# A third arm for expert slots of 33 to 64 rows: raw weights in two column tiles of 64

## The chip, the cores and the metric

The kernel runs on one core of one Trainium2 chip, as one program with one launch. The metric is the device time of an execution in microseconds (us).

## What is computed

Three blocks follow each other. The reference, cut to the block that the change touches:

```python
def reference(...):
    attn_out = _attn_ref(...)                      # (4, 8, 544, 64): local and global attention
    x = attn_out.transpose(0, 2, 1, 3).reshape(B, S, H * D)
    x = _moe_ref(x, w_gate, w_local, w1, w2)
    return _moe2_ref(x, w_in, conv_w, w_out)       # dense layer, convolution, gate, dense layer

def _moe_ref(x, w_gate, w_local, w1, w2):          # x (4, 544, 512), 8 experts
    logits = x @ w_gate
    local_gate = sigmoid(x @ w_local)
    for b in range(B):
        for s in range(S):
            e = argmax(logits[b, s]) if s == 0 or local_gate[b, s] < 0.5 else prev_e
            prev_e = e
            p = softmax(logits[b, s])
            h = maximum(x[b, s] @ w1[e], 0.0)      # w1[e] is 512 x 1024
            out[b, s] = p[e] * (h @ w2[e])         # w2[e] is 1024 x 512
```

All data are float32. There are 2,176 tokens. With the reference's inputs the experts 0 to 7 get 412, 308, 241, 397, 261, 158, 382 and 17 of them.

## The kernel before, in words

**The expert block.** After attention the routing sorts tokens by expert into *slots* of up to 128 rows. There are NSLOT = 25 slots, of which 22 are in use here. Slots 0 and 1 (NA = 2) are full slots of expert 0; their routing needs the first half of the tokens alone. The second routing phase (`phase_b`, L844) places the rest: the experts follow each other, and the first slot of each is the one that isn't full. Its rows stand at the end of the 128 rows, the last partitions. A small integer table `esi` holds per slot the expert, whether the expert changes there (row 1), what to load next (rows 2 and 3) and a flag for a short slot (row 5). `few` (L937) computes that flag on VectorE from the number of empty rows of each expert's first slot: 1 where at most 32 rows are filled.

**The order of the work.** `Moe.step` (L1452) is written out by hand. For slot s it issues, in this order: the flag of slot s + 1 (`small`, L1343), layer 1 of slot s (`layer1`, L1386), the load of the next layer 1 weights where an expert has begun (`fetch`, L1325), the gather of slot s + 3, the transposes of slot s + 1's rows (`turn_x`, L1354), a load of 512 columns of the third block's weights, the split of slot s + 1's layer 1 weights (`resplit`, L1337), layer 2 of slot s - 1 (`layer2`, L1439) with the scatter of its result, the load of the next layer 2 weights, the transposes of slot s's hidden rows (`turn_h`, L1424), and the split of slot s's layer 2 weights. Each engine works through its own part of this order. One piece per step of the third block's weights is converted from 64-bit storage between these (`convert`, L1487), on ScalarE, VectorE and GpSimd. The last of the step loop's slots goes through `last` (L1208).

**Two arms.** A full slot multiplies in three products of split numbers. A weight is a high part `wh` (a ScalarE cast) and a low part `wl` (a VectorE subtraction), and so are the rows (`xh`, `xl` and, for the hidden rows, `gh`, `gl`); L1110 and L1126 are the three products of layer 1 and layer 2, with the full 128 x 128 array and 512 columns per matmul. A short slot multiplies the raw float32 numbers instead, straight from the buffers `ws` in which the weights land. Its 32 rows take 32 columns of the array, so four groups of output columns run side by side: `few_l1` (L1399) issues 4 x 4 matmuls of 256 columns, `few_l2` (L1413) 8 x 4 of 128 columns, and `few_turn` (L1407) two transposes where a full slot has eight. `either` (L1348) is the branch between the two; it stands on the TensorE, ScalarE and VectorE queues:

```python
def either(self, s, few, all_):
    with self.tc.If(self.sm[s] != 0) as c:
        few()
    with c.Else():
        all_()
```

The weight buffers `ws` exist once per layer. A load into one waits for all that read it, the raw arm's matmuls and the split alike.

**Around the first slots.** While `phase_b` runs on VectorE, TensorE works on slots 0 and 1 (`fill`). `few` is called between the last comparison that builds the index matmul's operand and the computation of the gather indices. Slot 2 is the first of the second phase, and its transposed rows are prepared in both forms, since its flag is still on the way.

Of the kernel before, what the change touches and what calls it, by code (L numbers as in the profile page):

```python
# [13 lines left out]
ALU = mybir.AluOpType  # L14
# [3 lines left out]
P = 128  # L18
B, H, SL, SG, DH = 4, 8, 512, 32, 64
S = SL + SG  # L20
DM = H * DH
# [538 lines left out]
NA = 2  # L560
# [95 lines left out]
class Routing:  # L656
# [327 lines left out]
PAD_C, PAD_F = 104, 8  # L984
TS = 32
NTS = P // TS
NWARM_M = 10
# [65 lines left out]
class Moe:  # L1053
# [154 lines left out]
    def last(self, s, cwr, cw):  # L1208
# [20 lines left out]
        r = nc.values_load(self.rt.esi[0:1, 5, s:s + 1], min_val=0, max_val=1,  # L1229
                           engines=[mybir.EngineType.Activation, mybir.EngineType.DVE])  # L1230
# [6 lines left out]
        with self.tc.If(self.sm[s] != 0):  # L1237
            self.few_l1(xs, hp, hs)
        self.turn_h(p)
# [8 lines left out]
        tq = self.px.tile([P, 4, P], F32, tag="tr", name="hlq")  # L1248
        self.either(s, lambda: self.few_turn(hs, tq), full1)
        self.conv_w(cwr, cw)  # L1250
# [23 lines left out]

        self.either(s, lambda: self.few_l2(hs, yp, y), full2)
        resplit(4, NFC)
# [66 lines left out]
    def small(self, s):  # L1343
        self.sm[s] = self.nc.values_load(self.rt.esi[0:1, 5, s:s + 1], min_val=0, max_val=1,
                                         engines=[mybir.EngineType.PE, mybir.EngineType.Activation,
                                                  mybir.EngineType.DVE])

    def either(self, s, few, all_):  # L1348
        with self.tc.If(self.sm[s] != 0) as c:
            few()  # L1350
        with c.Else():
            all_()

    def turn_x(self, s):  # L1354
        nc = self.nc
        xs = self.xs[s]
        x = self.xt[s] = tuple(self.tp.tile([P, NKC, P], F32R, tag="x" + q, name="x" + q) for q in "hl")
        t = (self.ps if s == NA else self.px).tile([P, 4, P], F32, tag="tr", name="xlp")
# [5 lines left out]
        def few():  # L1364
            turn()
            raw()

        def raw():
            nc.scalar.copy(xs[:, 0:NKC * TS].rearrange("p (k t) -> p k t", t=TS), t[:, :, P - TS:P])

        def split():
            nc.scalar.copy(x[0], t)
            self.lo_t(x, 0, t)

        def full():
            turn()
            split()

        if s == NA:
            turn()  # L1380
            raw()
            split()
        else:
            self.either(s, few, full)

    def layer1(self, s):  # L1386
        nc, W = self.nc, self.W
        x, xs, hp = self.xt.pop(s), self.xs.pop(s), self.h_tile()
        hs = self.hs[s] = self.tp.tile([P, FF], F32, tag="hs", name="hs")

        def full():
            for k in range(NKC):
                self.l1_mm(x, W.t[1], hp, k, range(2))
            for c in range(2):
                self.relu_c(hp, hs, c)

        self.either(s, lambda: self.few_l1(xs, hp, hs), full)
# [9 lines left out]
    def few_turn(self, hs, t):  # L1407
        n = FF // NTS // P
        for a in range(n):
            self.nc.tensor.transpose(t[:, a, :], hs[:, P * a:P * a + P], self.ident)  # L1410
        self.nc.scalar.copy(hs[:, P * n:2 * P * n].rearrange("p (a t) -> p a t", t=P), t[:, 0:n])

    def few_l2(self, hs, yp, y):  # L1413
        n, w = FF // NTS // P, DM // NTS
        for k in range(NFC):
            j, a = divmod(k, n)
            o = P * (n + a) + TS * j
            for i in range(NTS):
                self.nc.tensor.matmul(yp[TS * i:TS * i + TS, 0:w], hs[:, o:o + TS], self.W.s[2][:, k, w * i:w * i + w],
                                      start=k == 0, stop=k == NFC - 1)  # L1420
        for i in range(NTS):
            self.nc.scalar.copy(y[P - TS:P, w * i:w * i + w], yp[TS * i:TS * i + TS, 0:w])

    def turn_h(self, s):  # L1424
# [11 lines left out]

        self.either(s, lambda: self.few_turn(hs, t[0]), full)

    def layer2(self, s):  # L1439
# [8 lines left out]

        self.either(s, lambda: self.few_l2(hs, yp, y), full)
        self.scatter(s, y)  # L1450
# [454 lines left out]
```

## Time and profile before

| | |
|---|---|
| time, median of 3 runs | 611.85 us (610.93 to 612.66) |
| the profiled execution's own time | 610.53 us |
| its span, first to last instruction | 608.6 us |
| TensorE busy, matmuls (share of the span) | 570.2 us (94%) |
| VectorE / ScalarE / GpSimd busy | 395.0 / 331.4 / 171.7 us |
| granted TensorE clock, mean | 0.986 |
| mean DMA rate | 149 GB/s |

The span is what the views of the trace cover; about 1.9 us of the execution's own time lie around it. PE is TensorE's matmul stream and PEld its weight loads, DVE is VectorE, ACT is ScalarE, POOL is GpSimd and SP is the queue that issues most DMAs. A trailing q (ACTq, DVEq, SPq) means the engine's sequencer: branches, register work, semaphores. A share of busy time averages over stages with different limits. Matmuls are pipelined, so the modelled durations of neighbouring ones overlap; the distance between starts tells their rate. Attention takes the first 150 us, the expert block lies between about 130 and 403 us, and the third block fills the rest. The fused copies of fp32 matmuls show as two records each.

### The profile page before, as it was taken

What the parts mean: (1) busy time and instruction counts of PE and PEld (TensorE: products, weight loads), DVE (VectorE), ACT (ScalarE), POOL (GpSimd) and SP (SyncE); (2) the same over time, 40 slices, a digit from 0 to 9 for tenths busy, and PEclk for the clock granted to TensorE, in tenths of its full rate; (3) what the DMA queues carried; (4) which work ended last, traced back from release to release, by engine and by line L of the source; (5) the groups of instructions that cost most, each with busy time, mean ns of one, the idle gap of its engine ahead of it and who ended that gap; (6) DMA issues with size and microseconds to landing.
All of it is one profiled execution on the core that took longest, in us unless ns stands there. A gap on an engine that the chain in (4) does not pass through costs nothing. (4 is left out here: it accounts for less than half of the span.)

```text
span 608.6 us, 16465 instructions
## 1 busy us (share of the span) xinstructions
PE 570.2 (94%) x6108; PEld 477.5 (78%) x6108; DVE 395.0 (65%) x821; ACT 331.4 (54%) x657; POOL 171.7 (28%) x226
## 2 busy tenths in 40 slices
PE   8789889879888999999999999889899999999997
PEld 7567667666666888887777788679898998998986
DVE  7877676865983857786487884457963574473330
ACT  5764555556324746865566774447762554463441
POOL 7655740025022332243142330010411403300100
PEclk9998999989899999999999999889999999999999
DMA  9989949656327964597366684321110210000001
GB/s 238 209 196 249 244 114 200 188 194 214 136 71 257 339 203 153 197 355 251 96 246 227 257 298 134 119 82 43 53 36 36 69 36 18 36 5 30 36 36 52
DMA packets 60644, 90.58 MB, mean 149 GB/s; under 512 B 25726, under 2 KB 34198, under 8 KB 60504
## 3 DMA queue, kind: packets, MB, share of 16 engines
q1 hardware_dynamic: 57016, 78.93, 42.5%
q0 software_dynamic: 3520, 10.23, 4.8%
q8 instruction: 65, 1.06, 0.8%
q14 instruction: 43, 0.35, 0.2%
HBM read 125.87 MB, written 15.79 MB: 233 GB/s over the span
## 5 line engine op out<-in xcount | busy, mean ns | idle before, releaser
L1608 DVE SCALAR_TENSOR_TENSOR fc<-f_hp,cw,fc 128x544 f32<-128x544 f32 (+2 forms) x66 | 51.4, 779 | 70.1 <-ACT fc L1606 68.7
L1046 DVE TENSOR_TENSOR wl<-ws,wh 128x512 fp32r<-128x512 f32 (+1 forms) x80 | 65.1, 874 | 16.5 <-ACT wh L1045 13.3
L1045 ACT CAST wh<-ws 128x512 fp32r<-128x512 f32 (+1 forms) x84 | 57.9, 772 | 2.8 <-DMA ws<-in_moe_w_dram 1.8
L1126 PE MATMUL yp<-wh,gh 128*128 128x512 f32 x136 | 55.9, 411 | 1.1 <-ACTq L1340 0.9
L1126 PE MATMUL yp<-wl,gh 128*128 128x512 f32 x136 | 54.8, 403 | 0.4 <-DVEq L1340 0.4
L1666 PE MATMUL f<-wh,fh 128*128 128x512 f32 (+1 forms) x144 | 54.8, 380 | 0.0
L1666 PE MATMUL f<-wh,fl 128*128 128x512 f32 (+1 forms) x144 | 54.4, 378 | 0.0
L1666 PE MATMUL f<-wl,fh 128*128 128x512 f32 (+1 forms) x144 | 54.4, 378 | 0.0
L1126 PE MATMUL yp<-wh,gl 128*128 128x512 f32 x136 | 54.4, 400 | 0.0
L278 ACT ACTIVATE pr<-sp,nm 128x128 f32<-128x128 f32 x128 | 36.6, 376 | 25.0 <-DVE nm L275 25.0
L1083 POOL DMA_INDIRECT y_dram<-ys,sidx x22 | 24.3, 1102 | 90.2 <-ACT ys L1447 30.2
L1110 PE MATMUL hp<-wl,xh 128*128 128x512 f32 x136 | 43.9, 394 | 2.1 <-DVEq L1340 1.1
L1110 PE MATMUL hp<-wh,xh 128*128 128x512 f32 x136 | 45.3, 405 | 0.4 <-PE hlp L1433 0.2
L1071 POOL DMA_INDIRECT xs<-x_dram,gidx x22 | 25.6, 1163 | 70.2 <-ACT pr L278 34.0
L1110 PE MATMUL hp<-wh,xl 128*128 128x512 f32 x136 | 43.6, 392 | 0.0
L1318 ACT ACTIVATE hs<-hp 128x512 f32<-128x512 f32 x34 | 18.7, 596 | 43.1 <-PE hp L1110 42.2
L1613 ACT ACTIVATE f_hp<-f 128x544 f32<-128x544 f32 x31 | 19.4, 624 | 34.7 <-PE f L1589 34.6
L1019 POOL TENSOR_TENSOR wf<-wf,fx 128x512 int32<-128x512 int32 x16 | 20.9, 1308 | 60.0 <-DVE wf L1018 54.7
L1675 ACT COPY fy<-f 128x512 f32<-128x512 f32 (+1 forms) x18 | 10.1, 564 | 46.6 <-PE f L1666 46.6
L1126 PEld LDWEIGHTS yp<-wh,gh 128*128 128x128 f32 x136 | 26.3, 193 | 8.4 <-issue 2.3
L1110 PEld LDWEIGHTS hp<-wl,xh 128*128 128x128 f32 x136 | 25.1, 188 | 9.0 <-DVEq L1340 2.1
L1666 PEld LDWEIGHTS f<-wh,fl 128*128 128x128 f32 x144 | 27.1, 188 | 5.1
(384 smaller groups left out, 1514.2 us busy)
## 6 DMA issues: line engine op xcount, KB each, us to landing
ws<-in_moe_w_dram SPq DMA_DIRECT2D x42, 2048.0 KB
fx<-y_dram SPq DMA_DIRECT2D x17, 256.0 KB
raw<-in_k_l_dram SPq DMA_DIRECT2D x16, 256.0 KB
x_dram<-x SPq DMA_DIRECT2D x16, 256.0 KB
fx<-in_moe_w_in_dram SPq DMA_DIRECT2D x8, 512.0 KB
fx<-in_moe_w_out_dram SPq DMA_DIRECT2D x8, 512.0 KB
out_dram<-fy SPq DMA_DIRECT2D x16, 256.0 KB
VA<-in_v_l_dram SPq DMA_DIRECT2D x20, 192.0 KB
```

Of the source, the lines that this page charges most:

```text
L278: nc.scalar.activation(pr[:, hp, :], sp[:, hp, :], AF.Exp, bias=nm[:, hp:hp + 1], scale=-1.0)
L1019: nc.gpsimd.tensor_tensor(a, a, lo, ALU.add)
L1045: (cp.tensor_copy if cp else self.nc.scalar.copy)(h, src[n][:, k, :])
L1046: eng.tensor_tensor(l, src[n][:, k, :], h.bitcast(F32), ALU.subtract)
L1071: self.nc.gpsimd.indirect_dma_start(out=xs, out_offset=None, in_=self.x_dram[0:n, :], in_offset=bass.IndirectOffsetOnAxis(ap=self.rt.gidx[ ...
L1083: self.nc.gpsimd.indirect_dma_start(out=self.y_dram[:, :], out_offset=bass.IndirectOffsetOnAxis(ap=self.rt.sidx[:, s:s + 1], axis=0), in_= ...
L1110: self.nc.tensor.matmul(hp[c], a[:, k, :], b[:, 512 * c:512 * c + 512], start=k == 0 and m == 0, stop=k == NKC - 1 and m == 2)
L1126: self.nc.tensor.matmul(yp, a[:, k, :], b, start=k == 0 and m == 0, stop=k == NFC - 1 and m == 2)
L1318: self.nc.scalar.activation(hs[:, 512 * c:512 * c + 512], hp[c], AF.Relu)
L1608: nc.vector.scalar_tensor_tensor(c[:, a:b], hp[:, a + t:b + t], self.cw[:, t, f:f + 1], c[:, a:b], ALU.mult, ALU.add)
L1613: self.nc.scalar.activation(hp[:, 1:S + 1].rearrange("p (a c) -> p a c", a=2), p[:, :, 0:272], AF.Relu)
L1666: self.nc.tensor.matmul(yp[:, cs], x[:, c], w[:, cs], start=f == 0 and n == 0, stop=f == NFC - 1 and n == 2)
```

## The change

`few` writes three values in place of two: 2 for slots with at most 32 rows (as before), 1 for 33 to 64 rows, 0 else. The fourth slot from the end gets only 2 or 0. `either` gets an inner branch, `part`, that picks between the 32-row and the 64-row form of the raw arm, for the slots up to NSLOT - 5. The 64-row form uses 64 columns of the array, two groups side by side: 4 x 2 matmuls of 512 columns in layer 1, four transposes, and 8 x 2 matmuls of 256 columns in layer 2. The raw copy of slot 2's rows, which is made before its flag is known, has 64 rows per piece in place of 32.

```diff
@@ few
-        v.tensor_scalar(sm, sm, P - TS - 0.5, 1024.0, ALU.is_lt, ALU.mult)
+        ks = tl([1, E], "r_ks")
+        v.tensor_scalar(ks, sm, P - TS - 0.5, 1.0, ALU.is_gt, ALU.add)
+        v.tensor_scalar(sm, sm, P - TM - 0.5, 1024.0, ALU.is_lt, ALU.mult)
         v.tensor_tensor(sm, sm, b0, ALU.add)
         eq = tl(sh, "r_s2")
         v.tensor_tensor(eq, sm[:, None, :].to_broadcast(sh), c.sl[0:1, :, None].to_broadcast(sh), ALU.is_equal)
+        v.tensor_tensor(eq, eq, ks[:, None, :].to_broadcast(sh), ALU.mult)
         v.tensor_reduce(self.esi[:, 5, NA:], eq, AX.X, ALU.max)
+        n = NSLOT - 4
+        v.tensor_scalar(self.esi[:, 5, n:n + 1], self.esi[:, 5, n:n + 1], 1, 2, ALU.is_gt, ALU.mult)
...
-TS = 32
-NTS = P // TS
+TS, TM = 32, 64
...
     def either(self, s, few, all_):
         with self.tc.If(self.sm[s] != 0) as c:
-            few()
+            self.part(s, few)
         with c.Else():
             all_()
+
+    def part(self, s, few):
+        if s > NSLOT - 5:
+            few(TS)
+            return
+        with self.tc.If(self.sm[s] != 1) as c:
+            few(TS)
+        with c.Else():
+            few(TM)
@@ turn_x
-        def raw():
-            nc.scalar.copy(xs[:, 0:NKC * TS].rearrange("p (k t) -> p k t", t=TS), t[:, :, P - TS:P])
+        def raw(ts):
+            nc.scalar.copy(xs[:, 0:NKC * ts].rearrange("p (k t) -> p k t", t=ts), t[:, :, P - ts:P])
...
         if s == NA:
             turn()
-            raw()
+            raw(TM)
             split()
...
-    def few_l1(self, xs, hp, hs):
-        w = FF // NTS
+    def few_l1(self, xs, hp, hs, ts, at=None):
+        m, at = P // ts, at or ts
+        w = FF // m
         for k in range(NKC):
-            for j in range(NTS):
-                self.nc.tensor.matmul(hp[0][TS * j:TS * j + TS, 0:w], xs[:, TS * k:TS * k + TS],
+            o = at * k + at - ts
+            for j in range(m):
+                self.nc.tensor.matmul(hp[0][ts * j:ts * j + ts, 0:w], xs[:, o:o + ts],
                                       self.W.s[1][:, k, w * j:w * j + w], start=k == 0, stop=k == NKC - 1)
         self.nc.scalar.activation(hs[:, 0:w], hp[0][:, 0:w], AF.Relu)
...
-    def few_l2(self, hs, yp, y):
-        n, w = FF // NTS // P, DM // NTS
+    def few_l2(self, hs, yp, y, ts):
+        n, m = FF * ts // P // P, P // ts
+        w = DM // m
         for k in range(NFC):
             j, a = divmod(k, n)
-            o = P * (n + a) + TS * j
-            for i in range(NTS):
-                self.nc.tensor.matmul(yp[TS * i:TS * i + TS, 0:w], hs[:, o:o + TS], self.W.s[2][:, k, w * i:w * i + w],
+            o = P * (n + a) + ts * j
+            for i in range(m):
+                self.nc.tensor.matmul(yp[ts * i:ts * i + ts, 0:w], hs[:, o:o + ts], self.W.s[2][:, k, w * i:w * i + w],
                                       start=k == 0, stop=k == NFC - 1)
...
```

What this makes of three places in the engines' instruction order (rows of equal instructions are merged; the line numbers shift by a few in the changed kernel).

VectorE in `few`, before: `r_sm` holds the number of empty rows by expert, then slot numbers; `r_s` is the comparison with all slots, `esi` the flag row, `r_iv` the first step of the gather indices.

```order
L941 SCALAR_TENSOR_TENSOR r_sm<-r_b_3695,r_nl 1x8
L942 TENSOR_SCALAR r_sm<-r_sm 1x8
L943 TENSOR_TENSOR r_sm<-r_sm,r_b_3695 1x8
L945 TENSOR_TENSOR r_s_3719<-r_sm,c_sl 1x184
L946 TENSOR_REDUCE esi<-r_s_3719 1x23
L883 TENSOR_SCALAR r_iv<-r_ip 128x23
```

The same place in the changed kernel:

```order
L941 SCALAR_TENSOR_TENSOR r_sm<-r_b_3695,r_nl 1x8
L943 TENSOR_SCALAR r_ks<-r_sm 1x8
L944 TENSOR_SCALAR r_sm<-r_sm 1x8
L945 TENSOR_TENSOR r_sm<-r_sm,r_b_3695 1x8
L947 TENSOR_TENSOR r_s_3721<-r_sm,c_sl 1x184
L948 TENSOR_TENSOR r_s_3721<-r_s_3721,r_ks 1x184
L949 TENSOR_REDUCE esi<-r_s_3721 1x23
L951 TENSOR_SCALAR esi<-esi 1x1
L883 TENSOR_SCALAR r_iv<-r_ip 128x23
```

Three instructions (L943, L948, L951) have come in ahead of the gather indices.

TensorE in `layer2` of a slot, before: `yp` is the result in PSUM, `ws` the raw weights, `hs` the hidden rows; the first matmul of the full arm stands last.

```order
L1340 UNCONDITIONAL_BRANCH
L1464 UNCONDITIONAL_BRANCH
L1349 COMPARE_AND_BRANCH
L1419 MATMUL yp<-ws_2725,hs 32x128 x32
L1349 UNCONDITIONAL_BRANCH
L1126 MATMUL yp<-wh_0_2734,gh 128x512
```

In the changed kernel:

```order
L1344 UNCONDITIONAL_BRANCH
L1485 UNCONDITIONAL_BRANCH
L1353 COMPARE_AND_BRANCH
L1362 COMPARE_AND_BRANCH
L1435 MATMUL yp<-ws_2725,hs 32x128 x32
L1362 UNCONDITIONAL_BRANCH
L1435 MATMUL yp<-ws_2725,hs 64x256 x16
L1362 UNCONDITIONAL_BRANCH
L1130 MATMUL yp<-wh_0_2734,gh 128x512
```

The narrow arm has an inner comparison ahead of it (L1362) and the 64-column arm behind it; the full arm is still reached by the outer comparison alone (L1353).

ScalarE between the split of slot s + 1's first weights and the casts of slot s's hidden rows, before: `ys` is the result of slot s - 1, copied from PSUM.

```order
L1349 COMPARE_AND_BRANCH
L1422 COPY ys_3455<-yp 32x128 x4
L1349 UNCONDITIONAL_BRANCH
L1447 COPY ys_3455<-yp 128x512
L1349 UNCONDITIONAL_BRANCH
L1349 COMPARE_AND_BRANCH
L1411 COPY hs<-hlp 128x256
L1349 UNCONDITIONAL_BRANCH
L1434 CAST gh<-hlp 128x512 x2
```

In the changed kernel, up to the same comparison (L1353, the last but two):

```order
L1353 COMPARE_AND_BRANCH
L1362 COMPARE_AND_BRANCH
L1443 COPY ys_3455<-yp 32x128 x4
L1362 UNCONDITIONAL_BRANCH
L1443 COPY ys_3455<-yp 64x256 x2
L1362 UNCONDITIONAL_BRANCH
L1468 COPY ys_3455<-yp 128x512
L1353 UNCONDITIONAL_BRANCH
L1353 COMPARE_AND_BRANCH
L1362 COMPARE_AND_BRANCH
L1426 COPY hs<-hlp 128x256
```

An inner comparison has come in ahead of the small slot's copies, and a second one ahead of the hidden rows' copy of a small slot.

## Rows read from the trace of the kernel before

**Rows 1.** Stages: us; busy (instructions) PE, PEld, DVE, ACT, POOL; clock; DMA share; GB/s.

```profile
208.70:221.00 12.30, 12.30 (x63) 10.23 (x61) 10.65 (x18) 8.67 (x18) 4.70 (x4) 1.00 0.52 183
221.00:390.00 169.00, 166.20 (x1063) 134.03 (x1062) 116.93 (x171) 109.51 (x191) 51.60 (x44) 1.00 0.62 216
```

**Rows 2.** ScalarE's activation behind the narrow layer 1: durations min/median/max, first and last start.

```profile
L1405 ACT ACTIVATE hs<-hp x5: 385/387/389, 183.1 to 387.3; 128x256 f32<-128x256 f32 x5
```

**Rows 3.** Timeline of TensorE around slot 4: start, us, instructions [idle before, releaser].

```profile
195.78 0.70 PE L1110 MATMUL hp<-wh,xh 128*128 128x512 f32 x2
...
201.94 0.60 PE L1362 MATMUL xlp<-ident,xs 128*128 128x128 f32 x4
202.29 0.48 PE L1126 MATMUL yp<-wh,gh 128*128 128x512 f32 x1
202.61 0.40 PE L1126 MATMUL yp<-wl,gh 128*128 128x512 f32 x1
...
214.59 0.48 PE L1126 MATMUL yp<-wh,gh 128*128 128x512 f32 x1
...
220.16 1.04 PE L1433 MATMUL hlp<-ident,hs 128*128 128x128 f32 x8
```

**Rows 4.** Timeline of TensorE, the narrow arm of slot 2.

```profile
180.95 1.93 PE L1403 MATMUL hp<-ws,xs 128*32 128x256 f32 x32 [0.40 <-ACT xs L1369]
182.81 0.65 PE L1362 MATMUL xlp<-ident,xs 128*128 128x128 f32 x4
...
192.46 2.16 PE L1419 MATMUL yp<-ws,hs 128*32 128x128 f32 x64
```

**Rows 5.** Timeline of ScalarE, VectorE and SP from 180 to 203 us.

```profile
180.58 0.27 ACT L1369 COPY xs<-xlp 128x128 f32<-128x128 f32 x1 [5.64 <-PE xlp L1362]
...
184.06 0.38 SPq L1038 DMA_DIRECT2D ws<-in_moe_w_dram  x1
...
194.45 3.89 ACT L1045 CAST wh<-ws 128x1024 fp32r<-128x1024 f32 x4 [0.93 <-DMA ws<-in_moe_w_dram]
198.58 1.06 ACT L1422 COPY ys<-yp 32x128 f32<-32x128 f32 x4 [0.24 <-ACTq L1464]
199.67 1.08 ACT L1434 CAST gh<-hlp 128x512 fp32r<-128x512 f32 x2
...
200.78 1.29 DVE L1103 TENSOR_TENSOR gl<-hlp,gh 128x512 fp32r<-128x512 f32 x2 [0.62 <-ACTq L1340]
```

**Rows 6.** Timeline of TensorE, the start of slot 1's layer 2.

```profile
175.13 0.50 PE L1126 MATMUL yp<-wh,gh 128*128 128x512 f32 x1 [0.86 <-ACTq L1340]
175.98 0.50 PE L1126 MATMUL yp<-wl,gh 128*128 128x512 f32 x1 [0.35 <-DVEq L1340]
```

**Rows 7.** Timeline of VectorE in the function that marks short slots, and behind it.

```profile
172.82 0.16 DVE L942 TENSOR_SCALAR r_sm<-r_sm 1x8 f32<-1x8 f32 x1
...
173.20 0.34 DVE L945 TENSOR_TENSOR r_s<-r_sm,c_sl 1x184 f32<-1x184 f32 x1
173.57 0.33 DVE L946 TENSOR_REDUCE esi<-r_s 1x23 int32<-1x184 f32 x1
...
174.48 1.29 DVE L1103 TENSOR_TENSOR gl<-hlp,gh 128x512 fp32r<-128x512 f32 x2
```

**Rows 8.** Timeline of TensorE, two other places where it stood idle.

```profile
45.92 0.41 PE L234 MATMUL trg<-ident,gn 128*128 128x128 f32 x2 [2.11 <-DMA gn<-in_k_g_dram]
...
390.38 0.16 PE L962 MATMUL lf<-c_ones,late 128*1 128x1 bf16 x1 [1.88 <-DVE esi L963]
```

**Rows 9.** Stretches behind idle places, with the granted clock (columns as in rows 1).

```profile
47.00:48.00 1.00, 1.00 (x30) 0.70 (x32) 1.00 (x3) 0.44 (x1) 0.94 (x2) 0.50 0.86 278
...
176.00:180.00 4.00, 4.00 (x18) 3.28 (x19) 3.63 (x25) 0.00 (x0) 1.97 (x2) 1.00 0.59 180
...
391.00:393.00 2.00, 2.00 (x7) 1.57 (x7) 0.00 (x0) 0.00 (x0) 0.00 (x0) 0.66 0.49 117
393.00:395.00 2.00, 2.00 (x6) 1.52 (x6) 0.76 (x2) 0.00 (x0) 0.00 (x0) 0.50 0.78 243
```

More of the change, by code (lines that the diff above doesn't have):

```diff
@@ L1227, in resplit @@
                     W.split_k(2, W.s, k, nc.vector)
-        r = nc.values_load(self.rt.esi[0:1, 5, s:s + 1], min_val=0, max_val=1,
+        r = nc.values_load(self.rt.esi[0:1, 5, s:s + 1], min_val=0, max_val=2,
                            engines=[mybir.EngineType.Activation, mybir.EngineType.DVE])
@@ L1237, in last @@
         with self.tc.If(self.sm[s] != 0):
-            self.few_l1(xs, hp, hs)
+            self.few_l1(xs, hp, hs, TS)
         self.turn_h(p)
@@ L1248, in last @@
         tq = self.px.tile([P, 4, P], F32, tag="tr", name="hlq")
-        self.either(s, lambda: self.few_turn(hs, tq), full1)
+        self.either(s, lambda ts: self.few_turn(hs, tq, ts), full1)
         self.conv_w(cwr, cw)
@@ L1273, in full2 @@
             split(K_LAST, NKC)
-        self.either(s, lambda: self.few_l2(hs, yp, y), full2)
+        self.either(s, lambda ts: self.few_l2(hs, yp, y, ts), full2)
         resplit(4, NFC)
@@ L1343, in small @@
     def small(self, s):
-        self.sm[s] = self.nc.values_load(self.rt.esi[0:1, 5, s:s + 1], min_val=0, max_val=1,
+        self.sm[s] = self.nc.values_load(self.rt.esi[0:1, 5, s:s + 1], min_val=0, max_val=2,
                                          engines=[mybir.EngineType.PE, mybir.EngineType.Activation,
@@ L1362, in turn, with few @@
                 nc.tensor.transpose(t[:, k, :], xs[:, P * k:P * k + P], self.ident)
-        def few():
+        def few(ts):
             turn()
-            raw()
-        def raw():
-            nc.scalar.copy(xs[:, 0:NKC * TS].rearrange("p (k t) -> p k t", t=TS), t[:, :, P - TS:P])
+            raw(ts)
+        def raw(ts):
+            nc.scalar.copy(xs[:, 0:NKC * ts].rearrange("p (k t) -> p k t", t=ts), t[:, :, P - ts:P])
         def split():
@@ L1380, in turn_x @@
             turn()
-            raw()
+            raw(TM)
             split()
@@ L1395, in full, with few_turn @@
                 self.relu_c(hp, hs, c)
-        self.either(s, lambda: self.few_l1(xs, hp, hs), full)
-    def few_l1(self, xs, hp, hs):
-        w = FF // NTS
+        self.either(s, lambda ts: self.few_l1(xs, hp, hs, ts, TM if s == NA else None), full)
+    def few_l1(self, xs, hp, hs, ts, at=None):
+        m, at = P // ts, at or ts
+        w = FF // m
         for k in range(NKC):
-            for j in range(NTS):
-                self.nc.tensor.matmul(hp[0][TS * j:TS * j + TS, 0:w], xs[:, TS * k:TS * k + TS],
+            o = at * k + at - ts
+            for j in range(m):
+                self.nc.tensor.matmul(hp[0][ts * j:ts * j + ts, 0:w], xs[:, o:o + ts],
                                       self.W.s[1][:, k, w * j:w * j + w], start=k == 0, stop=k == NKC - 1)
         self.nc.scalar.activation(hs[:, 0:w], hp[0][:, 0:w], AF.Relu)
-    def few_turn(self, hs, t):
-        n = FF // NTS // P
+    def few_turn(self, hs, t, ts):
+        n = FF * ts // P // P
         for a in range(n):
@@ L1411, in few_turn, with few_y @@
         self.nc.scalar.copy(hs[:, P * n:2 * P * n].rearrange("p (a t) -> p a t", t=P), t[:, 0:n])
-    def few_l2(self, hs, yp, y):
-        n, w = FF // NTS // P, DM // NTS
+    def few_l2(self, hs, yp, y, ts):
+        n, m = FF * ts // P // P, P // ts
+        w = DM // m
         for k in range(NFC):
             j, a = divmod(k, n)
-            o = P * (n + a) + TS * j
-            for i in range(NTS):
-                self.nc.tensor.matmul(yp[TS * i:TS * i + TS, 0:w], hs[:, o:o + TS], self.W.s[2][:, k, w * i:w * i + w],
+            o = P * (n + a) + ts * j
+            for i in range(m):
+                self.nc.tensor.matmul(yp[ts * i:ts * i + ts, 0:w], hs[:, o:o + ts], self.W.s[2][:, k, w * i:w * i + w],
                                       start=k == 0, stop=k == NFC - 1)
-        for i in range(NTS):
-            self.nc.scalar.copy(y[P - TS:P, w * i:w * i + w], yp[TS * i:TS * i + TS, 0:w])
+        if y is not None:
+            self.few_y(yp, y, ts)
+    def few_y(self, yp, y, ts):
+        w = DM * ts // P
+        for i in range(P // ts):
+            self.nc.scalar.copy(y[P - ts:P, w * i:w * i + w], yp[ts * i:ts * i + ts, 0:w])
     def turn_h(self, s):
@@ L1435, in full @@
                 self.lo_t(h, a, t[a // 4])
-        self.either(s, lambda: self.few_turn(hs, t[0]), full)
+        self.either(s, lambda ts: self.few_turn(hs, t[0], ts), full)
     def layer2(self, s):
@@ L1447, in full @@
             nc.scalar.copy(y, yp)
-        self.either(s, lambda: self.few_l2(hs, yp, y), full)
+        self.either(s, lambda ts: self.few_l2(hs, yp, y, ts), full)
         self.scatter(s, y)
```

## The prediction

> **What bounds the kernel now.** I began with busy time by stage: from 221 to 390 us, the later expert slots, TensorE is busy 166.2 of 169.0 us at full clock, and between 208.7 and 221 VectorE and ScalarE are busy 10.65 and 8.67 of 12.3 us [rows 1]. So a matmul taken away there shortens the run, as long as nothing else is late at that place. The question is therefore where the change takes matmuls away, and what is late there.
>
> Which slots are touched follows from the data. The experts get 412, 308, 241, 397, 261, 158, 382 and 17 tokens; two full slots of expert 0 are taken early, and each expert's remainder modulo 128 comes first in its slots. The remainders are 28, 52, 113, 13, 5, 30, 126 and 17 rows. Five are at most 32, as many as the narrow layer 1 ran [rows 2]. One alone lies between 33 and 64: expert 1 with 52 rows, its first slot, slot 4. All other slots keep their arm.
>
> Slot 4 stands in the timeline of TensorE [rows 3]: layer 1 from 195.78 to 201.94 (6.16 us), layer 2 from 214.59 to 220.16 (5.57 us). Four transposes take 0.35 us (201.94 to 202.29). Between its layers lies slot 3's layer 2, whose first two matmuls start at 202.29 and 202.61.
>
> **The new arm.** The narrow arm's layer 1 is 16 matmuls of 256 columns on four column tiles and takes 1.86 us (180.95 to 182.81); its layer 2, 32 matmuls of 128 columns, takes 2.16 us [rows 4]. Layer 2 of the new arm is again 16 matmuls of 256 columns, but on two tiles. Half the overlap means up to twice the time, 3.7 us; start and end are paid once, so I take 3.6 us. Ends: 2.16 us (the narrow arm's time) and 6.8 us (no overlap: four times the 1.7 us that remain of the 1.86 without start and end). Layer 1 has 8 matmuls of 512 columns, the same number of columns in all: also 3.6 us. Slot 4 needs four transposes of its hidden rows in place of eight, 0.35 us less. Counted on TensorE alone: 2.56 + 0.35 + 1.97 = **4.9 us less**.
>
> **What the shorter layer 1 runs into.** Slot 4 is the first slot with new weights, and their arrival sets the pace of the other engines. ScalarE waits for that DMA until 194.45, makes four casts (3.89 us), copies slot 2's result at 198.58, then casts slot 3's hidden rows from 199.67 to 200.75; VectorE makes their low halves from 200.78 to 202.07 [rows 5]. These wait for no matmul of slot 4. Slot 3's layer 2 needs the casts for its first matmul, and VectorE's work for its second. At the same hand-over for slot 1 VectorE ended at 175.77 (174.48 + 1.29) and TensorE went on at 175.98, 0.21 us later [rows 6, 7]; so slot 3's second matmul can start at 202.28, while it now starts at 202.61. Of the 2.56 us of layer 1 only **0.33 us** come through. What is late next is VectorE, behind ScalarE, behind the DMA. It also means that layer 1 may take up to six us at no cost, and only layer 2's size decides.
>
> **What the change adds ahead of that.** (a) Three VectorE instructions in the function that marks short slots, which stands ahead of the index computation and of slot 1's low halves. Prices: 0.16 us as the 1x8 operation, 0.37 us as the 1x184 one (173.20 to 173.57) and, for the 1x1, up to the 0.33 us of the reduction ahead of it [rows 7]. Narrow operations partly overlap, so I take 0.60 us in all, ends 0.5 and 0.9. No slack covers it: TensorE waited 0.35 us for VectorE in slot 1's layer 2 [rows 6]. The gathers and the reading of the flags are queued behind the same instructions and move along. (b) Slot 2's copy of raw rows has 256 columns in place of 128: 0.27 us now [rows 5], against 0.39 us for the 256-column one of layer 1 [rows 2]; TensorE waited 0.40 us for it [rows 4], so 0.11 us is added in full. Both precede slot 2's layer 1, which releases the weight buffer: the DMA of expert 1 goes out at 184.06 [rows 5] and would go out and land 0.71 us later. (c) The inner branch in small slots. On ScalarE it stands ahead of the copy of slot 2, where the existing block end and branch show 0.24 us of idle [rows 5]; I take 0.2 us, ends 0 and 0.3. So slot 3's second matmul moves to 202.28 + 0.71 + 0.2 = 203.19, **0.58 us later than now**.
>
> (d) On TensorE the inner branch is passed four times in each of slots 9, 13 and 16 too. By the row, leaving the narrow arm costs no idle: the transposes follow at 182.81, before the modelled end of the arm [rows 4]. I take 0.2 us for all, ends 0 and 2.9 (twelve times 0.24). [...] The full arm passes one outer branch as before, over a longer jump; I cost the full slots at nothing, since TensorE's work issued ahead covers the jumps of now (166.2 of 169.0 us busy [rows 1]). [...]
>
> **Sum without the clock:** +0.58 (slot 3's second matmul) - 0.35 (transposes) - 1.97 (slot 4's layer 2) + 0.2 (branches) = **-1.5 us**. After that VectorE keeps up by its share: 10.65 of 12.3 us now, less one low half of 1.29 us that the new arm drops [rows 1, 7], so 9.4 us of a slot that is 2.3 us shorter.
>
> **The clock.** With layer 1 done at about 200.1 (195.78 + 0.71 + 3.6) and the transposes at 200.45, TensorE stands until 203.19 but for one matmul: 2.5 us idle. [...] After the 0.86 and 0.35 us that slot 1's layer 2 waits [rows 6] it stayed at 1.00 from 176 to 180 [rows 9]. [...]
>
> **The forecast.** One fall: -1.5 + 1.6 = +0.1. Against the profiled execution's 610.53 us that is 610.6; the median of the runs stands 1.32 us above it, so the prediction is **611.9 us**: no change. About 0.3%, 1.8 us, is what a measurement of this kernel can tell from none, so faster means below 610.0 and slower above 613.7.
>
> **Rivals.**
> - *No fall* (0.22): the clock holds as it does behind slot 1's waits. 611.85 - 1.5 = 610.3. For it: a busy array right before; against it: both longer idle stretches [rows 8].
> - *Two falls* (0.18): the wait of slot 1's layer 2 tips the clock too: 611.9 + 1.6 = 613.5.
> - *TensorE isn't held* (0.12): the casts or the DMA get ahead, and all 4.9 us come through less 0.71 and 0.2: 611.85 - 4.0 = 607.9, with no fall. Against it: the DMA goes out no earlier and ScalarE works in order.
> - *The two tiles don't overlap* (0.05), the one that ends slower: layer 1 ends at 196.49 + 6.8 = 203.3, the transposes at 203.65, slot 3's layer 2 starts 1.36 us later than now, and slot 4's layer 2 grows by 1.26: +1.36 - 0.35 + 1.26 + 0.2 = +2.5, 614.3. It decides from 6.2 us for layer 1 on. [...]
> - *Uncovered branches* (0.03): (d) at 2.9 in place of 0.2: +2.7 on the forecast, 614.6.
> - That the arm isn't taken is excluded by the 52 rows unless the flag is wrong; its costs alone, 0.71 + 0.2, would leave +0.9 us: inside "no change".
>
> **How the numbers follow.** One fall has 0.40. Each case spreads by about 0.8 us (the runs before span 1.7). Faster: 0.12 + 0.4 of 0.22 + a little of the forecast = 0.23. Slower: 0.05 + 0.03 + 0.45 of 0.18 + a little = 0.18. Same: 0.59. The range leaves out the unheld case below and the last two above, and takes "no fall" and "two falls" with the bounds of (a) and (c): 609.2 to 614.2.
>
> **What would show it.** Right: sixteen records of 512 columns on 64 columns of the array near 196.5 us, then an idle TensorE of 2 us or more that ends on VectorE's low halves; VectorE's three instructions 0.6 us long; the weights landing 0.7 us later; layer 2 of slot 4 near 3.6 us; a granted clock of 0.5 behind 203 us. Wrong: slot 3's layer 2 following slot 5's transposes at once, or layer 2 of slot 4 above 5.5 us.

## The result, and the profile after

| | before | after |
|---|---|---|
| time, median | 611.39 us (4 runs, 608.71 to 612.66) | 616.39 us (4 runs, 614.65 to 621.83) |
| ratio, 95% interval | 1 | 1.010 (1.0061 to 1.0138) |
| the profiled execution, its span | 610.53, 608.6 us | 614.65, 612.9 us |
| TensorE from 221 to 390 us | 166.2 of 169.0 us busy | 162.6 of 169.0 us busy |

The change is slower by 1.0%, some 6 us; the forecast was no change, and the time lies above the range of 609.2 to 614.2.

The new arm itself does what was forecast. The timeline of TensorE around slot 4, after (start, us, instructions, in brackets the idle time before them and its releaser):

```profile
195.39 1.07 PE L1454 MATMUL hlp<-ident,hs 128*128 128x128 f32 x8 [1.12 <-ACT wh L1049]
196.77 3.65 PE L1418 MATMUL hp<-ws,xs 128*64 128x512 f32 x16 [0.31 <-PE hlp L1454]
200.36 0.66 PE L1375 MATMUL xlp<-ident,xs 128*128 128x128 f32 x4
201.58 0.47 PE L1130 MATMUL yp<-wh,gh 128*128 128x512 f32 x1 [0.56 <-ACT fx L1017]
201.88 0.39 PE L1130 MATMUL yp<-wl,gh 128*128 128x512 f32 x1
...
207.14 0.60 PE L1425 MATMUL hlp<-ident,hs 128*128 128x128 f32 x4
...
213.60 3.67 PE L1435 MATMUL yp<-ws,hs 128*64 128x256 f32 x32
217.20 1.09 PE L1454 MATMUL hlp<-ident,hs 128*128 128x128 f32 x8
```

Layer 1 takes 3.59 us (196.77 to 200.36) in place of 6.16, layer 2 3.60 us (213.60 to 217.20) in place of 5.57 [rows 3]. The two tiles overlap: the forecast's estimate for layer 1 without overlap was 6.8 us. Slot 5's hidden rows, which started at 220.16, start at 217.20, 2.96 us earlier; counted from slot 2's layer 1 (180.95 before, 180.54 after) it is 2.55 us.

Then it is lost. The transposes of hidden rows mark the slots: from 299.32 before to 298.47 after TensorE is still 0.85 us ahead, at the next such place (308.31 before, 311.10 after) 2.79 us behind, and at 360.48 against 364.36 it is 3.88 us behind. Behind the loss are seven idle places that the kernel before does not have: those at 195.39 and 201.58 above, and these five:

```profile
264.23 0.70 PE L1114 MATMUL hp<-wh,xh 128*128 128x512 f32 x2 [0.83 <-ACT hs L1426]
274.24 0.70 PE L1114 MATMUL hp<-wh,xh 128*128 128x512 f32 x2 [0.78 <-ACT fx L1017]
303.95 0.47 PE L1130 MATMUL yp<-wh,gh 128*128 128x512 f32 x1 [2.00 <-ACTq L1344]
351.97 0.70 PE L1114 MATMUL hp<-wh,xh 128*128 128x512 f32 x2 [1.58 <-ACT wh L1049]
358.83 0.47 PE L1130 MATMUL yp<-wh,gh 128*128 128x512 f32 x1 [0.72 <-ACT hs L1322]
```

Together the seven, called stops below, are 7.59 us. Each stands at the first matmul of a full arm, or of its transposes, behind a branch. The releasers named differ from place to place, and a conversion of the third block's weights (`fx`) cannot hold a layer of the expert block: the profile names the last event, not the cause. At 201.58 the casts and the low halves that the forecast waits for had been done, the later at 200.89 (timelines of ScalarE and VectorE):

```profile
198.48 1.07 ACT L1455 CAST gh<-hlp 128x512 fp32r<-128x512 f32 x2
199.60 1.29 DVE L1107 TENSOR_TENSOR gl<-hlp,gh 128x512 fp32r<-128x512 f32 x2 [0.70 <-ACTq L1344]
```

At the place of the 2.00 us the clock fell as well. The windows around the 2.00 us, where TensorE is busy 1.05 of 3.00 us and then slower (columns as in [rows 1]), and the DMA queues from 300.5 to 301.5 us (packets, MB, share):

```profile
302.00:305.00 3.00, 1.05 (x5) 0.91 (x6) 2.83 (x5) 0.98 (x3) 0.00 (x0) 0.99 0.75 225
304.00:306.00 2.00, 2.00 (x7) 1.65 (x8) 1.70 (x3) 0.88 (x2) 0.90 (x1) 0.74 0.97 391
306.00:308.00 2.00, 2.00 (x6) 1.54 (x6) 1.34 (x3) 0.54 (x1) 1.43 (x2) 0.50 1.03 410
308.00:310.00 2.00, 2.00 (x10) 1.62 (x9) 1.50 (x3) 0.00 (x0) 0.31 (x1) 0.91 0.98 363
```

```profile
q8 instruction: 1, 0.02, 8.2%
```

The fall costs 2 x 0.26 + 2 x 0.50 + 2 x 0.09 = 1.7 us. The last row is the clue: a packet of 16 KB that carries instructions begins there, at 300.96, and TensorE goes on 2.99 us later. The same holds at the other six places: one such packet begins in 192.5 to 193.5, 198.5 to 199.5, 260 to 261, 271 to 272, 348.5 to 349.5 and 356 to 357, and over all seven the idle time ends 2.54 to 3.62 us behind the begin of the packet. From slot 2's layer 1 to the matmul `lf` behind the last expert slots 34 packets begin (25 before); behind the other 27 no arm starts with an idle place of over 0.4 us. In the whole execution this queue moved 65 packets before:

```profile
q8 instruction: 65, 1.06, 0.8%
q14 instruction: 43, 0.35, 0.2%
```

and after:

```profile
q8 instruction: 74, 1.21, 0.9%
q14 instruction: 48, 0.39, 0.2%
```

The packets of q8 are of 16 KB each, those of q14 of 8 KB but for a few small ones. That TensorE stands at these branches until such a packet is there is the author's reading of the times; no view names a packet as what a stop waits for.

Counted from slot 2's layer 1 to `lf`, the change is 4.29 us longer (213.72 in place of 209.43). The terms above add up to about that: the gain of 2.55 us, which has the first two stops in it already, the other five with 5.91 us, and the fall with 1.7 us, less a wait of the kernel before that lies within the stop of 1.58 us:

```profile
349.41 0.73 PE L1110 MATMUL hp<-wl,xh 128*128 128x512 f32 x2 [0.67 <-DVE wl L1046]
```

-2.55 + 5.91 + 1.7 - 0.67 = 4.4 us.

### The profile page after: what moved, and what is told of

Same layout as the page of the kernel before. It is cut to its first block, busy times and chain, and to the rows that moved or that the text cites. A ratio compares the mean times of both kernels' runs of the same rounds, so it can differ in the third digit from the quotient of the medians.

```text
span 612.9 us, 16530 instructions
## 1 busy us (share of the span) xinstructions
PE 563.8 (92%) x6104; PEld 469.2 (77%) x6104; DVE 390.3 (64%) x821; ACT 330.5 (54%) x656; POOL 170.5 (28%) x226
## 5 line engine op out<-in xcount | busy, mean ns | idle before, releaser
L1130 PE MATMUL yp<-wh,gh 128*128 128x512 f32 x128 | 52.9, 413 | 4.7 <-ACTq L1344 2.9
L1130 PE MATMUL yp<-wl,gh 128*128 128x512 f32 x128 | 51.4, 402 | 0.9 <-DVEq L1344 0.9
L1130 PE MATMUL yp<-wh,gl 128*128 128x512 f32 x128 | 51.3, 401 | 0.0
L1114 PE MATMUL hp<-wh,xh 128*128 128x512 f32 x128 | 43.2, 409 | 3.2 <-ACT wh L1049 1.6
L1114 PE MATMUL hp<-wl,xh 128*128 128x512 f32 x128 | 41.4, 395 | 1.3 <-DVEq L1344 1.3
L1114 PE MATMUL hp<-wh,xl 128*128 128x512 f32 x128 | 41.2, 393 | 0.0
L1130 PEld LDWEIGHTS yp<-wh,gh 128*128 128x128 f32 x128 | 24.8, 194 | 12.4 <-issue 6.7
L1687 PEld LDWEIGHTS f<-wl,fh 128*128 128x128 f32 x144 | 27.1, 188 | 4.7
```

What stands on the lines that cost most here:

```text
L1114: self.nc.tensor.matmul(hp[c], a[:, k, :], b[:, 512 * c:512 * c + 512], start=k == 0 and m == 0, stop=k == NKC - 1 and m == 2)
L1130: self.nc.tensor.matmul(yp, a[:, k, :], b, start=k == 0 and m == 0, stop=k == NFC - 1 and m == 2)
L1687: self.nc.tensor.matmul(yp[:, cs], x[:, c], w[:, cs], start=f == 0 and n == 0, stop=f == NFC - 1 and n == 2)
```

## The experiments

Three theories were stated ahead of the first four runs: (A) TensorE's longer code, (B) the inner branch itself, (C) the added VectorE work and the wider copy. All runs stand in this table with the ratio to the kernel before on the same chip, the packets of the instruction queue q8, and the distance from slot 2's layer 1 to `lf`, read from the profile of each (180.95 to 390.38 before). That distance leaves out attention, whose length differs by some us from run to run. It is of one execution each; that of the TensorE part alone (221.14) was a long one, 624.1 us against a median of 618.09.

| run | ratio (95% interval) | q8 | slot 2 to lf, us |
|---|---|---|---|
| before | 1 | 65 | 209.43 |
| the change | 1.0100 (1.0061 to 1.0138) | 74 | 213.72 |
| flags and copy alone | 1.0026 (0.9996 to 1.0056) | 65 | 208.74 |
| inner branch, no third arm | 1.0028 (0.9993 to 1.0064) | 66 | 209.07 |
| third arm never taken | 1.0127 (1.0080 to 1.0175) | 74 | 212.46 |
| never taken, ScalarE part alone | 1.0017 (0.9990 to 1.0044) | 66 | 210.58 |
| never taken, TensorE part alone | 1.0126 (1.0079 to 1.0172) | 74 | 221.14 |
| of that, layer 2 alone | 1.0098 (1.0062 to 1.0134) | 71 | 214.74 |
| of that, all but layer 2 | 1.0120 (1.0076 to 1.0165) | 69 | 214.24 |
| TensorE part twice | 1.0530 (1.0471 to 1.0589) | 82 | 232.65 |
| the change, later code moved by 16 matmuls | 1.0170 (1.0115 to 1.0224) | 74 | 218.59 |
| moved by 32 | 1.0225 (1.0171 to 1.0279) | 75 | 222.72 |
| moved by 48 | 1.0181 (1.0121 to 1.0240) | 75 | 217.50 |
| the change, common transposes | 1.0122 (1.0064 to 1.0179) | 73 | 216.32 |
| third arm at slot 4 alone | 0.9972 (0.9938 to 1.0006) | 65 | 206.21 |
| slot 4 alone, common transposes | 0.9986 (0.9957 to 1.0015) | 65 | 208.46 |
| slot 4 alone, flags later | 1.0006 (0.9974 to 1.0039) | 65 | 207.78 |
| slot 4's narrow arm replaced | 0.9975 (0.9950 to 1.0000) | 65 | 206.37 |
| the same, moved by 16 | 0.9956 (0.9923 to 0.9990) | 65 | 206.20 |
| the same, moved by 48 | 1.0013 (0.9982 to 1.0043) | 65 | 208.56 |

### Code, branch or added work?

**The third arm at slot 4 alone.**

```diff
-        with self.tc.If(self.sm[s] != 0) as c:
+        with self.tc.If((self.sm[s] != 0) if s == NA + 2 else (self.sm[s] > 1)) as c:
...
-        if s > NSLOT - 5:
+        if s != NA + 2:
             few(TS)
```

> The 64-row arm exists at slot 4 alone; all other small slots keep the two arms of before. The theories: (A) code length: the third arm lies in the instruction stream of every slot, and TensorE stands while the code behind the jump is brought in; (B) the inner branch itself costs, at every pass; (C) the added VectorE work and the wider copy of slot 2 delay a hand-over, and that delay is paid. A and B: one slot of extra code and one inner branch, so nearly all of the loss goes and slot 4's gain stays: 1 to 3 us faster than the kernel before. C: the added work is all still there, so the loss stays: about 5 us slower than before, as the change.

**The third arm never taken**: the flag is 0 from 33 rows on.

```diff
-        v.tensor_scalar(sm, sm, P - TM - 0.5, 1024.0, ALU.is_lt, ALU.mult)
+        v.tensor_scalar(sm, sm, P - TS - 0.5, 1024.0, ALU.is_lt, ALU.mult)
```

> All code of the change is there, but the flag is never 1, so the third arm runs nowhere and slot 4 takes the full arm. Slot 4's gain of some 3 us falls away. A: 5 to 9 us slower than before, idle TensorE places whose named releaser had long been done. B: the same, 5 to 9 us slower. C: at most 1 us slower, since only 0.7 us of work was added ahead of slot 1's hand-over and the new arm's own waits are gone.

**The inner branch without the third arm**: the edit above, and

```diff
-        with self.tc.If(self.sm[s] != 1) as c:
+        with self.tc.If(self.sm[s] != 1):
             few(TS)
-        with c.Else():
-            few(TM)
```

> As the run in which the flag is never 1, but with the inner branch around the 32-row arm alone and no 64-row arm behind it: the branches of the change without its code. A: most of the loss goes, 0.3 to 1.5 us slower than before. B: the loss stays, 5 to 9 us slower. C: at most 1 us slower.

**Flags and copy alone**: the same with `few(TS)` and no inner branch.

> Only the three added VectorE instructions and slot 2's wider copy are left of the change: no inner branch, no third arm. A and B: 0.3 to 1 us slower than before (0.6 and 0.11 us by the rows). C: if these delays set off the loss, 3 us or more slower.

Measured: 1.0127 with the code there and never executed, 1.0028 with the branch and no code, 1.0026 with the flags and the copy alone, 0.9972 with the arm at slot 4 alone. (B) falls: the branches add nothing that can be told from flags and copy (the profile has one stop with them, 0.46 us at 267.87). (C) falls: what it names is all in the last two runs. (A) stands. With the arm never taken five of the seven idle places are there again, at the same starts of arms: the one of 195.39 at 193.72 (1.03 us), and these four, in the timeline of TensorE:

```profile
265.69 0.70 PE L1114 MATMUL hp<-wh,xh 128*128 128x512 f32 x2 [0.99 <-ACT hs L1426]
275.37 0.70 PE L1114 MATMUL hp<-wh,xh 128*128 128x512 f32 x2 [0.60 <-PE hlp L1454]
304.33 0.47 PE L1130 MATMUL yp<-wh,gh 128*128 128x512 f32 x1 [1.66 <-ACT xh L1385]
350.21 0.70 PE L1114 MATMUL hp<-wh,xh 128*128 128x512 f32 x2 [1.37 <-ACT wh L1049]
```

The releasers have changed (`hlp` for `fx`, `xh` for the queue), the places have not. None of these four stands in the run with the arm at slot 4 alone.

### Which engine, and how much code?

In the never taken arm, ScalarE's copies and the activation were left out (first run), or TensorE's matmuls and transposes (second run). For example, from the second:

```diff
-            for j in range(m):
+            for j in range(m if ts == TS else 0):
```

> As the run in which the flag is never 1, but of the 64-row arm only the TensorE instructions are left in the program; ScalarE has the inner branch with nothing behind it. If it is TensorE's own code that has to be brought in (A1): the loss stays whole, 5 to 8 us slower than before, with 74 packets on the instruction queue that grew from 65 to 74 with the change. If it is ScalarE's code, and TensorE waits for ScalarE (A2): 0.5 to 3 us slower.

> The other half: of the never executed 64-row arm only the ScalarE copies are left. A1: about as with the branches alone, 0.5 to 2.5 us slower than before, with 65 or 66 packets on the first instruction queue. A2: 5 to 8 us slower.

TensorE's part alone makes the whole loss (1.0126, 74 packets), ScalarE's part none that can be told (1.0017, 66 packets; its profile has two stops, of 0.66 and 0.67 us). That is what the expectations call A1; q8 grows with TensorE's code (74 packets) and not with ScalarE's (66, as with the inner branch alone), so it is taken for TensorE's queue. Next TensorE's part was cut in two and doubled.

> Of the never executed TensorE code only the 16 matmuls of layer 2 are left. If the price goes by the amount of code in all (A, by amount): half the added packets (69 or 70) and 2.5 to 4.5 us slower than before. If it goes by the single jump, whose target has to be there (A, by jump): idle places only at the start of layer 2, none at the start of layer 1; with one to two of them of 1 to 2 us, 1 to 4 us slower.

> The other part: never executed TensorE code in the transposes and in layer 1 (8 matmuls and 8 transposes per slot), none in layer 2. By amount: 69 or 70 packets and 2.5 to 4.5 us slower. By jump: idle places only at the start of layer 1, and 1.5 to 5 us slower.

> The never executed TensorE code of the 64-row arm stands twice in every slot. By amount: as many packets again, about 83, and twice the loss, 13 to 18 us slower than before. By jump: the same places become longer and others join them; anything over 10 us slower. If the loss has a ceiling (one fetch per slot hidden or not): 6 to 9 us slower, as with the code once.

The packets go by the amount (71, 69, 74, 82); the time does not. The two parts cost 0.98% and 1.20%, both together 1.26%, twice the code 5.3%. Nor is it the single longer jump: with code added everywhere but in layer 2, idle places appeared at layer 2, whose jump is longer by the inner branch alone:

```profile
266.30 0.39 PE L1130 MATMUL yp<-wh,gh 128*128 128x512 f32 x1 [2.92 <-ACT fx L1017]
286.76 0.50 PE L1130 MATMUL yp<-wh,gh 128*128 128x512 f32 x1 [1.36 <-ACTq L1344]
```

By amount the packets came nearly as expected (69 or 70 for either part, 83 for twice the code), and the time failed in all three. By jump failed with either part; for the doubled code it had anything over 10 us, and 5.3% is some 32 us.

### Amount or place?

The change with 16, 32 or 48 never executed matmuls more, all in slot 2's 64-row layer 1. All that follows lies that much further on, and no later jump is longer; only the one over them in slot 2 is (`r` is 2, 4 or 6 there and 0 elsewhere):

```diff
-        for k in range(NKC):
+        for k in list(range(NKC)) * (r + 1):
             o = at * k + at - ts
```

> The change, with 16 more never executed matmuls in one place, slot 2's 64-row layer 1. They lie ahead of all later slots in TensorE's code and move it by that much; every later jump keeps its length. By length of jump or amount: 4 to 6 us slower than before, as the change, with idle places at the same slots. By position (A, by position: what counts is whether a jump's target falls into a block that isn't there yet): idle places at other slots, and a time that differs from the change's by over 1.5 us, between 1 us faster and 10 us slower than before.

> The same with 32 more matmuls in that one place. By length or amount: 4 to 6 us slower than before, idle places at the same slots. By position: other slots, and a time that differs from that of the change or of the shift by 16 by over 1.5 us.

> The same with 48 more matmuls in that one place. By length or amount: 4 to 6 us slower than before, idle places at the same slots. By position: other slots, and a time that differs from at least one of the other shifts by over 1.5 us.

The loss goes from 1.0% to 1.70%, 2.25% and 1.81% with at most one packet more, and the idle places move. Clear of the noise against the unmoved change is the one moved by 32 alone; the intervals of the other two overlap with its. Moved by 16, the longest stop stands at the third matmul of its arm, and the profile shows nothing that TensorE waited for there ("issue"):

```profile
267.10 0.58 PE L1130 MATMUL yp<-wh,gl 128*128 128x512 f32 x1 [4.33 <-issue]
```

Moved by 32, two of the long ones, and the clock behind them:

```profile
205.88 0.76 PE L1130 MATMUL yp<-wh,gh 128*128 128x512 f32 x1 [3.84 <-ACTq L1344]
269.56 0.77 PE L1130 MATMUL yp<-wh,gh 128*128 128x512 f32 x1 [5.30 <-ACT fx L1017]
```

```profile
204.00:210.00 6.00, 4.12 (x10) 3.28 (x11) 4.81 (x9) 3.01 (x5) 2.19 (x2) 0.50 1.04 405
269.00:275.00 6.00, 5.44 (x13) 4.31 (x14) 2.65 (x5) 0.10 (x1) 2.34 (x2) 0.50 1.03 411
```

Here the packets begin at 203.2 and 266.9, when TensorE has stood since 202.04 and 264.26: part of a long stop lies ahead of the packet. In all runs with longer code the idle places of over 0.4 us at the starts of arms end 2.2 to 3.6 us behind the begin of a packet, but for the waits for casts and low halves.

So the loss depends on where the code lies and not only on how much of it there is. At the end of these two stops and behind it the granted clock was 0.50, from 204 to 210 and from 269 to 275 us, so they cost more than their own length (the first matmuls take 0.76 and 0.77 us in place of 0.47); behind the 2.92 us above it stayed at 1.00. Of the four places tried, the change as it stands has the lowest loss. Place isn't all that counts: the run with the third arm never taken and the one with TensorE's part alone have the same matmuls and transposes on TensorE, and the profiled executions show five stops of 5.65 us in one and seven of 9.53 us in the other, at nearly the same ratio. Whether that is timing or a few branches' difference in place is open.

**The change with common transposes.** The four transposes of a slot's rows are issued once ahead of the branch, in place of once per arm.

> The change with its third arm in all slots, but with the four transposes of the rows, which all three arms have in their own copy, issued once ahead of the branch: 8 transposes per slot less in TensorE's code. By amount: the loss shrinks by about a quarter, 3 to 4 us slower than before, and some 3 packets fewer than 74. By position: anything from 1 us faster to 7 us slower.

1.0122 with 73 packets: less code, no gain. By amount 3 to 4 us and some 71 packets were expected; 1.22% is 7.5 us, just above the range by position, which ended at 7. It speaks for place and against amount.

### A version without longer code

**Slot 4's narrow arm replaced.** Slot 4 gets the 64-row arm in the place of its narrow one, with one branch as before; its flag is set up to 64 rows. `NM` is 4. Against the change:

```diff
-        v.tensor_scalar(ks, sm, P - TS - 0.5, 1.0, ALU.is_gt, ALU.add)
-        v.tensor_scalar(sm, sm, P - TM - 0.5, 1024.0, ALU.is_lt, ALU.mult)
+        v.tensor_scalar(ks, b0, float(NM - NA), float(TM - TS), ALU.is_equal, ALU.mult)
+        v.tensor_tensor(sm, sm, ks, ALU.add)
+        v.tensor_scalar(sm, sm, P - TS - 0.5, 1024.0, ALU.is_lt, ALU.mult)
...
     def part(self, s, few):
...
+        few(TM if s == NM else TS)
```

> Slot 4 has the 64-row arm in the place of its 32-row arm, and its flag is set up to 64 rows; all other slots are as before, so there is no inner branch, no longer code anywhere, slot 2's copy stays narrow, and the marking grows by two 1x8 operations in place of three with one of 184 elements. If TensorE's code is what costs (A): 1.5 to 3.5 us faster than before, at least as good as the arm at slot 4 beside the narrow one. If the loss had another cause that the arm itself brings: 0 to 5 us slower.

**The same, moved** by 16 and by 48 matmuls that stand in slot 2's full layer 1, which isn't taken with these data.

> The 64-row arm in the place of slot 4's 32-row arm (no longer code), with 16 never executed matmuls added in one place, slot 2's full layer 1, so that all later code lies elsewhere. If the short jumps of two arms are safe wherever they lie: as without the shift, 0 to 3 us faster than before, no new idle places from 221 to 385 us. If the kernel before only lies well: over 1.5 us slower than before.

> The same with 48 never executed matmuls there. Safe wherever they lie: 0 to 3 us faster than before. If the kernel before only lies well: over 1.5 us slower than before in this run or in the one with 16.

0.9975, 0.9956 and 1.0013: none is slower than before, and no new idle place of over 0.4 us at the start of a full arm appears from 221 to 385 us in either moved version. Clear of the noise faster than before is the one moved by 16 alone. The one moved by 48 came out 0.1% slower, where 0 to 3 us faster had been expected. Its profile shows another reason than code: slot 3's layer 2 waits 0.99 us for ScalarE's queue and 0.79 us for VectorE's, and the clock falls behind it, as the prediction expected there:

```profile
202.00:204.00 2.00, 1.62 (x6) 1.30 (x7) 1.50 (x4) 1.63 (x3) 0.00 (x0) 0.85 1.05 376
204.00:206.00 2.00, 2.00 (x6) 1.53 (x5) 1.93 (x4) 0.27 (x1) 0.27 (x1) 0.50 1.05 394
206.00:208.00 2.00, 2.00 (x9) 1.60 (x7) 1.57 (x3) 1.16 (x2) 1.84 (x2) 0.80 1.03 414
```

That is 2 x 0.15 + 2 x 0.50 + 2 x 0.20 = 1.7 us of the 2.19 us by which its distance is above the unmoved one's.

From slot 2 to `lf` the unmoved version is 3.06 us shorter than before. Of this 1.25 us are given back where the third block starts: from `lf` to its first matmul it takes 15.45 us (385.36 to 400.81) in place of 14.20. Its timeline there, and the clock behind:

```profile
385.36 0.16 PE L965 MATMUL lf<-c_ones,late 128*1 128x1 bf16 x1 [1.84 <-DVE esi L966]
400.81 0.57 PE L1603 MATMUL f<-f_x0h,wh 128*128 128x272 f32 x1 [2.91 <-PEq L1200]
```

```profile
402.00:404.00 2.00, 2.00 (x11) 2.00 (x10) 1.97 (x4) 0.00 (x0) 0.00 (x0) 0.50 0.59 122
```

The kernel before waits 1.63 us there, and the two moved versions take 14.40 and 14.11 us. TensorE jumps over the code of the leftover slots at this place, and a packet of instructions begins within 397 to 400 us; that this wait is the same thing was argued from that and not tried apart.

**Two more on the way.** With the arm at slot 4 alone, the transposes were made common, or the function that marks short slots was called behind the index computation.

```diff
-                self.few(b0, nl)
...
         yield "idx"
+        self.few(b0, nl)
```

> The 64-row arm at slot 4 alone, and the four transposes of the rows, which both arms have in their own copy, are issued once ahead of the branch, so TensorE's code becomes shorter than that of the kernel before, and it has one branch fewer per slot. If code length is what costs (A), fewer packets on TensorE's instruction queue than 65, and 0.5 to 2 us faster than the arm at slot 4 alone, so 2 to 4 us faster than before. If a code that is short enough costs nothing (a limit rather than a price per block): the same as the arm at slot 4 alone, 1 to 2.5 us faster than before.

> The 64-row arm at slot 4 alone, and the function that marks short slots is called behind the computation of the gather and scatter indices instead of ahead of it. Its eight VectorE instructions (about 1.5 us) no longer stand ahead of the gathers. If slot 1's wait for VectorE is on the path (0.84 us with the arm at slot 4 alone): 0.5 to 1 us faster than the run with the arm at slot 4 alone, 2 to 3 us faster than before. If the marking only moves, with the low halves still behind it, or if the weights of expert 1 arrive no earlier: the same as the arm at slot 4 alone, 1 to 2.5 us faster than before.

Shorter code brought no further gain, with the packets still 65 (0.9986): where no jump stops TensorE, still less code gained nothing that can be measured. (In its profiled execution the clock fell behind slot 3's wait, to 0.82, 0.50 and 0.82 in the three stretches of 2 us from 200 on.) The later flags lost what they were to bring (1.0006). Slot 1's wait for VectorE went from 0.84 to 0.71 us only, and slot 2's layer 1 waited longer:

```profile
182.75 2.79 PE L1417 MATMUL hp<-ws,xs 128*32 128x256 f32 x24 [2.30 <-DMA ws<-in_moe_w_dram]
```

With the arm at slot 4 alone it waited 0.51 us. The granted clock around it was 0.68 from 182 to 184 and 0.50 from 184 to 186. Whether it is the flag or the weights that came late is open.

## Why the prediction was wrong, point by point

- **Full slots at nothing: the step that failed.** It read "I cost the full slots at nothing, since TensorE's work issued ahead covers the jumps of now". That holds for the jumps of now: none of the seven idle places stands in the kernel before. With the third arm's code in between there are seven stops of 0.56 to 2.00 us, 7.59 us together, and 1.7 us of lower clock, and five of the seven places stay with the arm never taken. That work issued ahead is what covers a jump was an estimate from 166.2 of 169.0 us busy; that number is of the present code and tells nothing of a longer one.
- **(d) The inner branch, 0.2 us.** It holds as far as the runs can tell: branch, flags and copy together 1.0028, flags and copy alone 1.0026. The rival "uncovered branches" at 614.6 gave a time near the measured one by the wrong mechanism: it put a price on each branch of the small slots, and the stops are in full slots.
- **The new arm, 3.6 us per layer.** 3.59 and 3.60 us. The four transposes take 0.35 us (207.14 to 207.49), the eight took 0.79 (207.87 to 208.66): 0.44 us less, forecast 0.35. In the rival of tiles that don't overlap, layer 2 grows by 6.8 - 5.57 = 1.23 us and not 1.26; its 614.3 stands.
- **(a) and (b).** Slot 1's second matmul waited 0.94 us in place of 0.35, so 0.59 against 0.60 forecast; slot 2's raw copy 0.51 in place of 0.40, so 0.11 as forecast. The three instructions of VectorE (L943, L948, L951), after:

```profile
171.70 0.16 DVE L943 TENSOR_SCALAR r_ks<-r_sm 1x8 f32<-1x8 f32 x1
...
172.64 0.34 DVE L948 TENSOR_TENSOR r_s<-r_s,r_ks 1x184 f32<-1x184 f32 x1
...
173.38 0.14 DVE L951 TENSOR_SCALAR esi<-esi 1x1 int32<-1x1 int32 x1
173.45 0.16 DVE L883 TENSOR_SCALAR r_iv<-r_ip 128x23 f32<-128x23 f32 x1
```

- **What is late behind the shorter layer 1: right in kind, off by 1.0 us.** With the arm at slot 4 alone, where no stop covers it, slot 3's layer 2 waits for ScalarE's queue and then VectorE's, as forecast:

```profile
180.72 1.93 PE L1418 MATMUL hp<-ws,xs 128*32 128x256 f32 x32 [0.51 <-ACT xs L1382]
...
199.99 0.47 PE L1130 MATMUL yp<-wh,gh 128*128 128x512 f32 x1 [0.40 <-ACTq L1344]
201.24 0.50 PE L1130 MATMUL yp<-wl,gh 128*128 128x512 f32 x1 [0.78 <-DVEq L1344]
```

  The two waits are 1.18 us, where 2.5 us of idle had been forecast. The second matmul starts 20.52 us behind slot 2's layer 1; forecast were 203.19 - 180.95 - 0.71 = 21.53. The weights of expert 1 allowed the first cast 12.79 us behind that layer (193.51) where the execution of before had 13.50; with flags and copy alone it was 12.85. The prediction took one execution's arrival for the rule. In the change itself that matmul starts 21.34 us behind (201.88), near the forecast by luck: the stops at 195.39 and 201.58 hold it, and VectorE's low halves had been done at 200.89.
- **The clock fall behind it: came in some versions.** The granted clock was 1.00 from 200 to 204 us with the arm at slot 4 alone (waits of 0.40 and 0.78 us), and from 203 to 205 us after. It fell with the short version moved by 48 (0.99 and 0.79 us) and with slot 4 alone and common transposes (0.66 and 0.79 us), at 1.7 us each; with the later flags it stayed at 1.00 behind 1.38 and 0.77 us. The 1.6 us that the forecast adds for one fall stands in no run: these two falls and the one behind the stop of 2.00 us cost 1.7 us each, as does the one from 391 to 395 before, 2 x 0.34 + 2 x 0.50 = 1.7 us [rows 9]; those of the run moved by 32 are longer. So the forecast's fall and the rival "no fall" (-1.5 us) both occur, and these runs don't tell which waits bring it. With the arm at slot 4 alone it is the rival: with the 1.0 us above its forecast would be -1.5 - 1.0 = -2.5 us in all, -3.2 counted from slot 2 on without (a) and (b). Measured there is 206.21 - 209.43 = -3.2 us.
- **The range** was built from the places that the change edits. Nothing in it stood for code that no slot executes.

## What to carry to other kernels

A branch arm that is never taken wasn't free here: with TensorE's part of it in the program and never executed the kernel was 1.26% slower, with ScalarE's part alone 0.17%, which can't be told from nothing. Compare the packets of the instruction queue before and after (65 and 74 here); idle places of TensorE at the first matmuls behind a branch, with a different releaser each time or none ("issue"), were the sign. Put a special arm only where the data need it: at one slot, beside the narrow arm (0.9972) or in its place (0.9975), it brought no loss. When a kernel has such stops, move its code by a few never executed instructions before believing a difference of about one per cent.

## What the runs showed of the hardware that was not expected

A DMA queue that the profile shows, q8, carries instructions in packets of 16 KB and grows with TensorE's code (65 before, 82 with the never taken code twice), and the stops of TensorE at the starts of arms ended 2.2 to 3.6 us after such a packet began. Nine packets more are 0.15 MB; what costs is up to 5.30 us of standing still at one jump, and the granted clock of 0.50 behind it (269 to 275 us, moved by 32). The same code at four places, up to 48 matmuls apart, lost between 1.00% and 2.25%. What sets when a packet begins, and so which place is a good one, was not found out.
